# Making the rounded part and the remainder of an activation one group later

## The chip, the cores and the metric

The kernel runs on one core of a Trainium2 chip. A core has a matrix engine (TensorE, PE in the rows, its weight loads PEld), a vector engine (VectorE, DVE), a scalar engine (ScalarE, ACT), GpSimd (POOL) and SyncE (SP), which here only starts transfers. Each engine works through its own queue in order and waits there for the others. The metric is the device time of one execution in microseconds, as the median of several runs. The kernel before took 430.98 us (median of 3 runs, 430.86 to 431.17).

## The reference

A recurrent attention (gates, a running matrix state per head, a normalised read-out) is followed by a two-layer network on its output. Only the network's activation is touched by the change.

```python
# attention, per time step t, for 4 batches and 8 heads, 768 steps, head size 40
C = f_stab * C + i_stab * outer(v_t, k_t)          # state 40x40
n = f_stab * n + i_stab * k_t
y_t = sigmoid(o_t) * (C @ q_t) / max(|n . q_t|, 1)
# network on the 3072 rows of 320 features
h = x @ w_in                                       # 320 -> 2048
g = h * (1.0 / (1.0 + np.exp(-h)))
return (g @ w_out).astype(np.float32)              # 2048 -> 320
```

## The kernel before, in words

The attention is cut into 24 units (12 chunks of 64 time steps, two pairs of batches). Three units make one step of the network, so there are 8 steps, called step 0 to step 7 here as `j` in the code. A step has 384 rows and goes over the 2048 hidden features in 16 groups of 128 (`fc`). While step j of the network runs, the three units of step j+1 are computed in between: `PLACES` says behind which groups their matrix work, the "block", stands (groups 2, 7 and 12 in step 1, groups 0, 4 and 8 in later ones). Step 7 has no units left to compute beside it.

Precision is kept by splitting a value in two parts that TensorE reads at full rate: a rounded part ("hi", type fp32r) and the remainder ("lo"). From step 1 on both layers use three products of such parts. For one group of step j:

- `mm1` (L849): 8 matmuls into `ph`, one of two PSUM buffers.
- `act`: ScalarE makes `th = tanh(ph/2)` (L856), VectorE makes `th = (th + 1) * ph` (L871), ScalarE rounds it to `gh` (L876), VectorE makes the remainder `gl = th - gh` (L880). `th` has two buffers, `gh` and `gl` three each.
- `mm2` (L901): for each of three row tiles three matmuls, gh with hi weights, gh with lo weights, gl with hi weights. It runs two groups behind (`LAG = 2`): the queue of TensorE is mm1(fc), the block if there is one, mm2(fc-2), mm1(fc+1), mm2(fc-1) and so on.

In step 1 `act` also carries pieces of the splitting of the weights (`splits`, L316 to L328): a rounding on ScalarE and a subtraction on VectorE (L318 for w_out, 640 columns, L327 for w_in, 512 columns), up to two in a group. Where a group has a block, a marker on ScalarE stands behind the tanh, for which the second half of the block's L637 matmuls waits, and VectorE has the weighting and the norm (`close`, L576, L655 to L660) ahead of the remainder. Two and three groups behind a block stand, on VectorE, the additions to the state (L757), on ScalarE the gate (L522) and the exponential `lq` (L529), and on GpSimd the multiplication `qt` (L533) that waits for `lq`; later the split of the transposed rows (`xh` on ScalarE L805, `xl` on VectorE L806).

The order on every engine is the order in which the code is written; the scheduler is set to manual for all of them. In step 7 the last group's mm2 order is written out at the end of the program: the three last groups, 13, 14 and 15, one row tile at a time, in the order (13,0) (14,0) (13,1) (14,1) (13,2) (15,0) (15,1) (14,2) (15,2). The rows of a tile are halved and stored right behind it (L919, L921, L926).

Of the kernel before, what the change touches and what calls it, by code (L numbers as in the profile page):

```python
# [8 lines left out]
F32 = mybir.dt.float32  # L9
# [5 lines left out]
ALU = mybir.AluOpType  # L15
# [10 lines left out]
NFC = DFF // 128  # L26
# [3 lines left out]
NSTEP = NU // UPS  # L30
# [13 lines left out]
def mlstm_mlp_kernel(  # L44
# [12 lines left out]
    nc = tc.nc  # L57
# [23 lines left out]
    for k in range(2):  # L81
        m = mask[k * L : (k + 1) * L]
        nc.gpsimd.affine_select(
            out=m, in_=m, compare_op=ALU.is_ge, fill=NEG, base=0,
# [79 lines left out]
    def gates(lo, hi):  # L164

        init = NEG if lo == 0 else m_t[:, lo - 1 : lo]
        nc.vector.tensor_tensor_scan(
            m_t[:, lo:hi], f_t[:, lo:hi], i_t[:, lo:hi], init, op0=ALU.add, op1=ALU.max
        )
        yield  # L170
        l1 = max(lo, 1)
        tt = nc.vector.tensor_tensor
        tt(out=f_t[:, l1:hi], in0=f_t[:, l1:hi], in1=m_t[:, l1 - 1 : hi - 1], op=ALU.add)
        yield
        tt(out=f_t[:, l1:hi], in0=f_t[:, l1:hi], in1=m_t[:, l1:hi], op=ALU.subtract)
        nc.vector.tensor_scalar(f_t[:, l1:hi], f_t[:, l1:hi], -120.0, None, op0=ALU.max)
        if lo == 0:
            nc.vector.memset(f_t[:, 0:1], 0.0)
        yield
        nc.vector.tensor_tensor_scan(  # L180
            LF[:, lo:hi], pat[:, lo:hi], f_t[:, lo:hi], 0.0, op0=ALU.mult, op1=ALU.add
        )
        yield
        tt(out=i_t[:, lo:hi], in0=i_t[:, lo:hi], in1=m_t[:, lo:hi], op=ALU.subtract)
        tt(out=i_t[:, lo:hi], in0=i_t[:, lo:hi], in1=LF[:, lo:hi], op=ALU.subtract)
        yield
# [196 lines left out]
    class Unit:  # L383
# [412 lines left out]
        def xput(self, st):  # L796
# [10 lines left out]
                out=lo, in0=px[:, a, :], in1=hi.bitcast(F32), op=ALU.subtract  # L807
            )

    class Step:  # L810


# [40 lines left out]
        def act(self, fc, splits=(), first=lambda: None, between=lambda: None):  # L853
            j, ph = self.j, self.ph
            th = p2.tile([128, NT], F32, tag="th", name=f"th{j}_{fc}")
            nc.scalar.activation(th, ph, AF.Tanh, scale=0.5)  # L856
            first()
            for x in splits:
                next(x)
            if j == 0:  # L860

                g = p3.tile([128, NT], F32, tag="gh", name=f"g{j}_{fc}")
                nc.vector.scalar_tensor_tensor(
                    out=g, in0=th, scalar=1.0, in1=ph, op0=ALU.add, op1=ALU.mult
                )
                self.g[fc] = (g, None)
                for x in splits:
                    next(x, None)
                between()
                return  # L870
            nc.vector.scalar_tensor_tensor(  # L871
                out=th, in0=th, scalar=1.0, in1=ph, op0=ALU.add, op1=ALU.mult
            )
            gh = p3.tile([128, NT], F32R, tag="gh", name=f"gh{j}_{fc}")
            gl = p3.tile([128, NT], F32R, tag="gl", name=f"gl{j}_{fc}")
            nc.scalar.copy(gh, th)  # L876
            for x in splits:
                next(x, None)
            between()
            nc.vector.tensor_tensor(  # L880
                out=gl, in0=th, in1=gh.bitcast(F32), op=ALU.subtract
            )
            self.g[fc] = (gh, gl)

        def mm2(self, fc, tiles=range(UPS)):
            j = self.j
# [117 lines left out]
    late = [gates(4 * L, 8 * L), gates(8 * L, S)]  # L1004
# [253 lines left out]
```

## Time and profile before

| | us |
|---|---|
| median of the timed runs | 430.98 |
| profiled execution | 431.02 |
| its span, first to last instruction | 429.2 |
| PE busy (5062 matmuls) | 422.4 (98%) |
| PEld busy | 391.7 (91%) |
| DVE busy | 288.5 (67%) |
| ACT busy | 220.6 (51%) |
| POOL busy | 124.8 (29%) |

The shares are means over the whole span. TensorE is busy nearly throughout; the other engines are busier in the first third than later. What counts for a change on the other engines is whether TensorE, which works through its queue without a pause, finds `gh`, `gl` and a free `ph` when it comes to them.

### The profile page before, as it was taken

Reading aid. Unit: us, or ns where it says so; the run is one execution under the profiler, and the core shown is the slowest. Engines: PE = TensorE matmul, PEld = TensorE weight load, DVE = VectorE, ACT = ScalarE, POOL = GpSimd, SP = SyncE. Lnnn points to the kernel's source line nnn. Section 1 sums busy time; section 2 is a strip of 40 time slices with the busy share of each in tenths; the row PEclk is TensorE's granted clock in tenths of the full one; section 3 lists DMA queues with packets and bytes.
Section 4 is the critical chain, followed back from the end, with each engine's and each line's share of the span. In section 5 each row is a group of like instructions: output and inputs, shape, how many; then the busy total and the mean of one; then the engine's idle time right before and its main releaser. Section 6 shows DMA issues by size and latency. Waiting matters only on the chain.

```text
span 429.2 us, 12518 instructions
## 1 busy us (share of the span) xinstructions
PE 422.4 (98%) x5062; PEld 391.7 (91%) x5062; DVE 288.5 (67%) x650; ACT 220.6 (51%) x481; POOL 124.8 (29%) x135
## 2 busy tenths in 40 slices
PE   8999999999999999999999999999999999999995
PEld 4767677899999999999999999999999999999995
DVE  5888799877887677467765677566764756443342
ACT  7684866755755454454454644444454543353331
POOL 5734135234234423043412344034320400000000
PEclk9999999999999999999999999999999999999999
DMA  8999696334551775127660575316750231001001
GB/s 272 387 366 311 177 299 165 117 89 141 159 169 21 196 196 155 31 61 189 174 172 2 123 218 139 118 25 179 209 163 22 54 94 20 18 9 39 2 2 46
DMA packets 62650, 57.17 MB, mean 133 GB/s; under 512 B 31440, under 2 KB 49184, under 8 KB 62592
## 3 DMA queue, kind: packets, MB, share of 16 engines
q1 hardware_dynamic: 62288, 55.94, 45.7%
q8 instruction: 40, 0.66, 0.7%
q10 hardware_dynamic: 208, 0.26, 0.2%
q0 software_dynamic: 96, 0.16, 0.1%
q14 instruction: 18, 0.15, 0.1%
HBM read 48.99 MB, written 7.36 MB: 131 GB/s over the span
## 4 chain that ended last, share of the span: by engine, by line
PE 80%; issue 17%; DVE 1%; ACT 1%; POOL 0%; POOLq 0%; ACTq 0%; DVEq 0%
PE ph L849 35%; PE pout L901 33%; PE p L549 3%; PE p L637 2%; PE p L620 2%; PE dummy L999 1%; PE pu_u L705 1%; PE pu_h L705 1%; DVE D L576 0%; PE e L396 0%; PE px L794 0%; PE pu L717 0%; PE po L604 0%; PE p L794 0%; POOL qt L533 0%
## 5 line engine op out<-in xcount | busy, mean ns | idle before, releaser
L856 ACT ACTIVATE th<-ph 128x384 f32<-128x384 f32 x128 | 62.4, 488 | 106.7 <-PE ph L849 106.2
L849 PE MATMUL ph<-xh,wh 128*128 128x384 f32 x336 | 113.8, 339 | 0.0
L849 PE MATMUL ph<-xl,wh 128*128 128x384 f32 x336 | 113.6, 338 | 0.0
L901 PE MATMUL pout<-woh,gh 128*128 128x320 f32 x336 | 105.5, 314 | 0.0
L901 PE MATMUL pout<-woh,gl 128*128 128x320 f32 x336 | 103.9, 309 | 0.0
L901 PE MATMUL pout<-wol,gh 128*128 128x320 f32 x336 | 103.3, 307 | 0.0
L876 ACT CAST gh<-th 128x384 fp32r<-128x384 f32 x112 | 57.5, 513 | 81.3 <-DVE th L871 69.9
L880 DVE TENSOR_TENSOR gl<-th,gh 128x384 fp32r<-128x384 f32 x112 | 64.6, 577 | 47.5 <-ACT gh L876 47.5
L871 DVE SCALAR_TENSOR_TENSOR th<-th,ph 128x384 f32<-128x384 f32 x112 | 61.4, 548 | 51.1 <-ACT th L856 50.6
L849 PE MATMUL ph<-xh,wl 128*128 128x384 f32 x224 | 75.9, 339 | 0.0
L747 POOL TENSOR_TENSOR Cm<-Cm,lq 40x328 f32<-40x328 f32 x40 | 30.6, 764 | 114.6 <-PE p L637 111.8
L901 PEld LDWEIGHTS pout<-woh,gh 128*128 128x128 f32 x336 | 63.0, 188 | 0.9
L849 PEld LDWEIGHTS ph<-xh,wh 128*128 128x128 f32 x336 | 63.1, 188 | 0.2
L849 PEld LDWEIGHTS ph<-xl,wh 128*128 128x128 f32 x336 | 63.0, 188 | 0.2
L901 PEld LDWEIGHTS pout<-woh,gl 128*128 128x128 f32 x336 | 63.0, 188 | 0.1
L901 PEld LDWEIGHTS pout<-wol,gh 128*128 128x128 f32 x336 | 63.1, 188 | 0.0
L533 POOL TENSOR_TENSOR qt<-qk,lq 104x512 f32<-104x512 f32 x22 | 29.7, 1348 | 99.4 <-ACT lq L529 89.3
L849 PEld LDWEIGHTS ph<-xh,wl 128*128 128x128 f32 x224 | 42.1, 188 | 0.0
L901 PE MATMUL pout<-wo,g 128*128 128x320 f32 x96 | 28.7, 435 | 0.0
L516 POOL TENSOR_TENSOR D<-D,am 128x512 f32<-128x512 f32 x20 | 26.1, 1303 | 4.0 <-DMA D<-LFd 2.5
L508 POOL TENSOR_TENSOR am<-mask,aT 128x512 f32<-128x512 f32 x20 | 24.1, 1205 | 6.6 <-DVE aT L207 5.1
L576 DVE TENSOR_TENSOR D<-p,D 128x512 f32<-128x512 f32 x24 | 16.5, 689 | 13.7 <-PE p L637 12.3
(136 smaller groups left out, 524.4 us busy)
## 6 DMA issues: line engine op xcount, KB each, us to landing
qk<-in_qk_dram SPq DMA_DIRECT2D x24, 512.0 KB, 5.1
ko<-in_ko_dram SPq DMA_DIRECT2D x24, 320.0 KB, 5.3
wro<-in_w_out_dram SPq DMA_DIRECT2D x8, 640.0 KB, 7.3
D<-LFd SPq DMA_DIRECT2D x40, 128.0 KB, 3.1
lq<-LFd SPq DMA_DIRECT2D x40, 128.0 KB, 4.9
wri<-in_w_in_dram SPq DMA_DIRECT2D x8, 512.0 KB, 6.0
vb<-in_vp_dram SPq DMA_DIRECT2D x48, 82.0 KB, 5.1
out_dram<-ob SPq DMA_DIRECT2D x45, 80.0 KB, 2.1
```

What stands on the lines that cost most here:

```text
L508: nc.gpsimd.tensor_tensor(out=self.am, in0=mask.unsqueeze(1).broadcast_to([128, H, L]), in1=aT[:, self.c, self.p, :].unsqueeze(2).broadcas ...
L516: nc.gpsimd.tensor_tensor(out=self.Dm, in0=self.Dm, in1=self.am, op=ALU.add)
L533: nc.gpsimd.tensor_tensor(out=self.qt, in0=self.q[:KS], in1=self.lq[:KS], op=ALU.mult)
L549: nc.tensor.matmul(self.ps[d * L : (d + 1) * L, a * 4 + j, :], self.k[r, d * 4 + j, :], self.q[r, d * 4 + j, :], start=True, stop=True,)
L576: nc.vector.tensor_tensor(out=self.Dm, in0=self.ps, in1=self.Dm, op=ALU.mult)
L747: nc.gpsimd.tensor_tensor(out=v, in0=v, in1=self.lq[r, :, L - 1].unsqueeze(2).broadcast_to([D, H, D1]), op=ALU.mult,)
L849: nc.tensor.matmul(ph, w, x, start=(i == 0), stop=(i == len(ops) - 1))
L856: nc.scalar.activation(th, ph, AF.Tanh, scale=0.5)
L871: nc.vector.scalar_tensor_tensor(out=th, in0=th, scalar=1.0, in1=ph, op0=ALU.add, op1=ALU.mult)
L876: nc.scalar.copy(gh, th)
L880: nc.vector.tensor_tensor(out=gl, in0=th, in1=gh.bitcast(F32), op=ALU.subtract)
L901: nc.tensor.matmul(self.po[t], g[:, ts], w, start=(fc == 0 and i == 0), stop=(last and i == len(ops) - 1),)
```

## The change

For every group of steps 1 to 7 the instructions that make `gh` and `gl` are no longer issued behind the group's own tanh and activation, but behind those of the next group. A list `behind` holds the one group that waits. The pieces of the weight splitting and the block's `close` stay in the group in which they were, between the two. The last group of the program has no next one: there both pairs are made in a row, group 14's and then group 15's. TensorE's queue and the number of instructions stay as they are.

```diff
--- before.py
+++ after.py
@@ -807,6 +807,8 @@
                 out=lo, in0=px[:, a, :], in1=hi.bitcast(F32), op=ALU.subtract
             )
 
+    behind = []
+
     class Step:
 
 
@@ -871,16 +873,26 @@
             nc.vector.scalar_tensor_tensor(
                 out=th, in0=th, scalar=1.0, in1=ph, op0=ALU.add, op1=ALU.mult
             )
+            self.late(splits, between)
             gh = p3.tile([128, NT], F32R, tag="gh", name=f"gh{j}_{fc}")
             gl = p3.tile([128, NT], F32R, tag="gl", name=f"gl{j}_{fc}")
-            nc.scalar.copy(gh, th)
+            self.g[fc] = (gh, gl)
+            behind[:] = [(th, gh, gl)]
+            if j == NSTEP - 1 and fc == NFC - 1:
+                self.late()
+
+        def late(self, splits=(), between=lambda: None):
+            waiting = behind.pop() if behind else None
+            if waiting:
+                th, gh, gl = waiting
+                nc.scalar.copy(gh, th)
             for x in splits:
                 next(x, None)
             between()
-            nc.vector.tensor_tensor(
-                out=gl, in0=th, in1=gh.bitcast(F32), op=ALU.subtract
-            )
-            self.g[fc] = (gh, gl)
+            if waiting:
+                nc.vector.tensor_tensor(
+                    out=gl, in0=th, in1=gh.bitcast(F32), op=ALU.subtract
+                )
 
         def mm2(self, fc, tiles=range(UPS)):
             j = self.j
```

On VectorE in step 1, around group 9, the kernel before has these instructions (`gl_8` is the remainder of group 8, `th_9` the activation of group 9, `wl` a piece of the weight splitting, `Cm` the state, `xl` the split of transposed rows):

```order
L880 TENSOR_TENSOR gl_8_1723<-th_8_1717,gh_8_1722 128x384
L757 TENSOR_TENSOR Cm_139<-Cm_139,pu_u 40x164
L757 TENSOR_TENSOR Cm_139<-Cm_139,pk_1683 40x164
L757 TENSOR_TENSOR Cm_139<-Cm_139,pu_u 40x164
L757 TENSOR_TENSOR Cm_139<-Cm_139,pk_1683 40x164
L806 TENSOR_TENSOR xl_1496<-px_1530,xh_1495 128x3x128
L871 SCALAR_TENSOR_TENSOR th_9_1765<-th_9_1765,ph_9_1756 128x384
L327 TENSOR_TENSOR wl_1767<-wi_1014,wh 128x512
L880 TENSOR_TENSOR gl_9_1771<-th_9_1765,gh_9_1770 128x384
```

The changed kernel has there, with line numbers shifted by the added lines:

```order
L893 TENSOR_TENSOR gl_7_1680<-th_7_1601,gh_7_1679 128x384
L757 TENSOR_TENSOR Cm_139<-Cm_139,pu_u 40x164
L757 TENSOR_TENSOR Cm_139<-Cm_139,pk_1681 40x164
L757 TENSOR_TENSOR Cm_139<-Cm_139,pu_u 40x164
L757 TENSOR_TENSOR Cm_139<-Cm_139,pk_1681 40x164
L806 TENSOR_TENSOR xl_1494<-px_1528,xh_1493 128x3x128
L873 SCALAR_TENSOR_TENSOR th_9_1763<-th_9_1763,ph_9_1754 128x384
L327 TENSOR_TENSOR wl_1765<-wi_1014,wh 128x512
L893 TENSOR_TENSOR gl_8_1724<-th_8_1715,gh_8_1723 128x384
```

The remainder of group 8 has moved past the state's four additions, the split `xl`, the activation of group 9 and a piece of the weight splitting; where it stood is now the remainder of group 7.

At the end of the program ScalarE has this queue in the kernel before (`ob` is an output tile):

```order
L856 ACTIVATE th_14_6192<-ph_14_6183 128x384
L876 CAST gh_14_6195<-th_14_6192 128x384
L856 ACTIVATE th_15_6217<-ph_15_6208 128x384
L876 CAST gh_15_6220<-th_15_6217 128x384
L921 ACTIVATE ob_6242<-pout_0_5896 128x320
```

and this one in the changed kernel:

```order
L858 ACTIVATE th_14_6190<-ph_14_6181 128x384
L888 CAST gh_13_6170<-th_13_6165 128x384
L858 ACTIVATE th_15_6215<-ph_15_6206 128x384
L888 CAST gh_14_6195<-th_14_6190 128x384
L888 CAST gh_15_6220<-th_15_6215 128x384
L933 ACTIVATE ob_6242<-pout_0_5894 128x320
```

The rounding of group 14 now stands behind the tanh of group 15. VectorE's last instructions are in the changed kernel:

```order
L873 SCALAR_TENSOR_TENSOR th_14_6190<-th_14_6190,ph_14_6181 128x384
L893 TENSOR_TENSOR gl_13_6171<-th_13_6165,gh_13_6170 128x384
L873 SCALAR_TENSOR_TENSOR th_15_6215<-th_15_6215,ph_15_6206 128x384
L893 TENSOR_TENSOR gl_14_6196<-th_14_6190,gh_14_6195 128x384
L893 TENSOR_TENSOR gl_15_6221<-th_15_6215,gh_15_6220 128x384
```

Here too group 14's remainder comes behind the activation of group 15; before, it stood ahead of it.

## Rows read from the trace of the kernel before

**Rows 1.** Waits of TensorE over the span: engine, line, releaser: total, times, longest
```profile
PE dummy L999 <- POOL ident masks.py:199: 1.4, 1, 1.4
...
```
**Rows 2.** Timeline, step 7: group 1's tanh and activation, group 0's first remainder matmul
```profile
382.62 0.49 ACT L856 ACTIVATE th<-ph 128x384 f32<-128x384 f32 x1 [1.10 <-PE ph L849]
...
383.15 0.56 DVE L871 SCALAR_TENSOR_TENSOR th<-th,ph 128x384 f32<-128x384 f32 x1 [1.03 <-ACT th L856]
...
385.38 0.31 PE L901 MATMUL pout<-woh,gl 128*128 128x320 f32 x1
```
**Rows 3.** Timeline, step 1, group 9 on ACT, DVE, POOL; group 8's mm2
```profile
109.74 0.49 ACT L856 ACTIVATE th<-ph 128x384 f32<-128x384 f32 x1 [0.54 <-PE ph L849]
110.12 0.61 ACT L325 CAST wh<-wi 128x512 fp32r<-128x512 f32 x1
111.78 0.51 ACT L876 CAST gh<-th 128x384 fp32r<-128x384 f32 x1 [1.04 <-DVE th L871]
...
112.57 0.62 ACT L529 ACTIVATE lq<-lq 104x512 f32<-104x512 f32 x1
...
111.19 0.55 DVE L871 SCALAR_TENSOR_TENSOR th<-th,ph 128x384 f32<-128x384 f32 x1
111.66 0.69 DVE L327 TENSOR_TENSOR wl<-wi,wh 128x512 fp32r<-128x512 f32 x1
112.32 0.56 DVE L880 TENSOR_TENSOR gl<-th,gh 128x384 fp32r<-128x384 f32 x1
...
113.26 1.30 POOL L533 TENSOR_TENSOR qt<-qk,lq 104x512 f32<-104x512 f32 x1 [4.92 <-ACT lq L529]
...
112.49 0.31 PE L901 MATMUL pout<-woh,gl 128*128 128x320 f32 x1
```
**Rows 4.** Timeline, step 1, group 14 on DVE; group 13's mm2
```profile
127.70 0.82 DVE L318 TENSOR_TENSOR wol<-wo,woh 128x640 fp32r<-128x640 f32 x1
128.43 0.55 DVE L880 TENSOR_TENSOR gl<-th,gh 128x384 fp32r<-128x384 f32 x1
...
128.53 0.31 PE L901 MATMUL pout<-woh,gl 128*128 128x320 f32 x1
```
**Rows 5.** Timeline, the end: group 15 on ACT and DVE, PE's last matmuls
```profile
420.80 0.49 ACT L856 ACTIVATE th<-ph 128x384 f32<-128x384 f32 x1 [1.10 <-PE ph L849]
421.91 0.51 ACT L876 CAST gh<-th 128x384 fp32r<-128x384 f32 x1 [0.62 <-DVE th L871]
...
421.32 0.56 DVE L871 SCALAR_TENSOR_TENSOR th<-th,ph 128x384 f32<-128x384 f32 x1 [1.04 <-ACT th L856]
422.45 0.56 DVE L880 TENSOR_TENSOR gl<-th,gh 128x384 fp32r<-128x384 f32 x1 [0.58 <-ACT gh L876]
...
420.97 0.31 PE L901 MATMUL pout<-woh,gh 128*128 128x320 f32 x1
...
422.73 0.31 PE L901 MATMUL pout<-woh,gh 128*128 128x320 f32 x1
...
423.32 0.31 PE L901 MATMUL pout<-woh,gh 128*128 128x320 f32 x1
```
**Rows 6.** Timeline, steps 0 and 3: DVE beside POOL's multiplication qt
```profile
76.74 2.17 POOL L533 TENSOR_TENSOR qt<-qk,lq 104x512 f32<-104x512 f32 x1 [4.71 <-ACT lq L529]
...
76.99 0.66 DVE L327 TENSOR_TENSOR wl<-wi,wh 128x512 fp32r<-128x512 f32 x1
...
204.36 1.30 POOL L533 TENSOR_TENSOR qt<-qk,lq 104x512 f32<-104x512 f32 x1 [4.22 <-ACT lq L529]
...
204.72 1.36 DVE L806 TENSOR_TENSOR xl<-px,xh 128x384 fp32r<-128x384 f32 x1 [0.74 <-ACT xh L805]
```
**Rows 7.** Timeline, step 3, the block of group 8: tanh and the two L637 halves
```profile
207.53 0.47 ACT L856 ACTIVATE th<-ph 128x384 f32<-128x384 f32 x1
...
207.79 0.42 PE L637 MATMUL p<-Cm,qt 40*64 40x41 f32 x16
...
208.35 0.44 PE L637 MATMUL p<-Cm,qt 40*64 40x41 f32 x16
```

## Prediction

> **What bounds the kernel now.** I read the waits of TensorE first, then the timelines of the steady last step, of step 1 and of the end. The view of waits should tell you whether anything is to be won: its longest entry for TensorE is 1.4 us, at the very start of the program [rows 1], and no entry names `gh`, `gl` or `ph`. TensorE works from its first matmul to its last without waiting for the activation. So freeing ScalarE and VectorE from waits for each other can win nothing by itself, and what remains to be asked is whether TensorE, under the new order, comes to a part of the activation before it is made.
>
> That is a question of distance. mm2(fc) stands behind mm1(fc+2). Before, gh(fc) and gl(fc) are made right behind mm1(fc), so two groups of TensorE's work cover them. Afterwards they come behind the tanh and the activation of group fc+1, with one group as cover. The steps of the change then differ only in how much else stands in that one group.
>
> **The change part by part.** Nothing is added or removed but order: the same roundings and remainders, with the same durations. ScalarE's rounding loses its wait for VectorE, since the activation it reads is a group old; VectorE's remainder loses its wait for the rounding for the same reason. Neither is on TensorE's path, so I carry both at nothing. The buffers: tanh(fc+2) needs the `th` that gl(fc) reads, which it gets as soon as mm2(fc) gets gl(fc) itself; it is not a second term.
>
> *Steady groups.* In step 7 the tanh of group 1 starts at 382.62 and its activation at 383.15 [rows 2]. The next VectorE instruction, now gl(0), can start about 0.47 behind the start of an activation (111.19 to 111.66 in [rows 3]) and takes 0.56: it ends at 384.18. TensorE wants it at 385.38 [rows 2], or a weight load earlier. That leaves about 1 us, and gh(0), done behind the tanh at 383.5, has more. The 13 groups of step 7 whose mm2 stands in the loop cost nothing, nor do the like ones of steps 2 to 6, where I read group by group that the remainder still comes in time; behind the `xl` of those steps, the closest place, ScalarE now runs the gate and `lq` about half a microsecond sooner, which brings the next activation forward.
>
> *What a late part costs.* The end of the program shows one small wait already: gl(15) ends at 422.45 + 0.56 = 423.01, and the matmul behind the one that waits for it starts at 423.32, that is 0.31 after the end [rows 5]. The unhindered pitch is (422.73 - 420.97)/12 = 0.147 us per matmul [rows 5], so that matmul would have stood at 422.73 + 4 x 0.147 - in other words, the wait before is 423.32 - (422.73 + 0.44) = 0.15 us. I use the same rule for new waits: next matmul = end of the part + 0.31.
>
> *Step 1, group 8.* VectorE is full here: state additions, `xl`, the activation of group 9 and a piece of the weight splitting run back to back, and gl(8) now stands at the end of that row, where gl(9) was: 112.32, ending at 112.88 [rows 3]. TensorE wants it at 112.49 [rows 3], the matmul behind at 112.64. It gets there at 112.88 + 0.31 = 113.19: 0.55 us lost. As VectorE has work without a gap up to there, the freed waits do not bring it forward (0.06 at most, the start of the piece at 111.66 plus some 0.6).
>
> *Step 1, group 13.* The same picture behind the next block: gl(13) takes the place of gl(14), 128.43 to 128.98, behind the piece that starts at 127.70 [rows 4]. TensorE wants it at 128.53, the matmul behind at 128.68, and comes to that at 129.29: 0.61 us. Other groups of step 1 have the same row of work with more time around it; some are on time only by tenths, and I carry them at nothing.
>
> *The end.* The tail of TensorE begins with the three matmuls of (13,0), then (14,0) at 420.97 [rows 5]. Before, group 14 was long done by then. Now gh(14) stands behind the tanh of group 15: that starts at 420.80, the next ScalarE instruction can follow 0.38 later (109.74 to 110.12 in [rows 3]), at 421.18, and with 0.51 ends at 421.69. TensorE, 0.31 behind that, starts the second matmul of (14,0) at 422.00 in place of 421.12: 0.88 lost. The third one needs gl(14), which VectorE makes behind the activation of group 15: start 421.32 + 0.47 = 421.79, end 422.35, next matmul at 422.66 in place of 420.97 + 0.44 = 421.41. So the tail is 1.25 us late from there on. gh(15) and gl(15) end as before, at 422.42 and 423.01; TensorE now comes to them at 422.66 + 9 x 0.147 = 423.98, so the old wait of 0.15 goes. Net: 1.25 - 0.15 = 1.10 us. Everything behind it (halving, stores) hangs on TensorE's last matmuls and moves along. A bound from below: none of it can be hidden, as TensorE has only these 27 matmuls left.
>
> *The sum.* 0.55 + 0.61 + 1.10 = 2.26 us. Against the profiled execution's 431.02 us that gives 433.3 us; it stands 0.04 above the median of the timed runs, so I predict 433.2 us. What TensorE loses anywhere is lost for good, since it has no waits into which a delay could vanish.
>
> *The port of VectorE and GpSimd.* One cost is open in step 1. The `xl` of step 3 starts 0.36 after GpSimd's `qt` and takes 1.36 us in place of some 0.56, ending 0.42 after `qt` ends at 205.66 [rows 6]: a VectorE instruction with two inputs in SBUF is held up by it. In step 1 `qt` moves too: it follows `lq`, which follows the rounding, and the rounding no longer waits for the activation. gh(8) can start at about 110.12 + 0.52 = 110.64; before, `lq` came 0.79 behind the rounding's start and `qt` 0.69 behind that [rows 3], so `qt` starts at about 112.12 in place of 113.26, and gl(8) follows at 112.32, 0.20 later. In step 0 a piece of the weight splitting that started 0.25 after `qt` took its plain 0.66, and `qt` took 2.17 instead of 1.30 [rows 6]. 0.20 is nearer to 0.25 than to 0.36, so I take gl(8) as not held up. If it is, it ends at 112.12 + 1.30 + 0.42 = 113.84 in place of 112.88: 0.96 us more, and as much again behind group 13, which has the same instructions.
>
> The Trainium skill, page "SBUF — State Buffer", section "Who interferes with whom", says that a VectorE instruction with two SBUF inputs and a GpSimd instruction that reads SBUF share a port pair as an exclusive lock: whichever issues first has it for its whole instruction and the other fully blocks. The `xl` row agrees with that; the row of step 0, where the later one by its recorded start ran unhindered, does not if recorded starts are taken as issue order. By that rule `qt`, started first, would hold gl(8), and the sum would be 3.2 us for one place and 4.2 us for both.
>
> **The rivals.**
>
> *GpSimd gets the port first.* In one or both of the places of step 1 the remainder is held up by `qt`: 431.0 + 2.26 + 0.96 = 434.2 us, or 435.2 us with both. For it speaks the `xl` row and that my start of `qt` has an uncertainty of a tenth; against it the row of step 0 and that the piece ahead of gl(8) still runs when `qt` arrives.
>
> *Only the end costs.* VectorE reaches gl(8) and gl(13) early enough, say because the subtraction ahead of them has its input sooner, and only the 1.10 us of the tail remain: 432.1 us. Against it: VectorE's row there has no gap in [rows 3] that could close.
>
> *Not slower: a hidden wait in the blocks goes.* The second L637 half of a block waits for a marker on ScalarE behind the tanh. In step 3, group 8, the tanh runs from 207.53 to 208.00, late because ScalarE had waited for VectorE; the first half of L637 ends at 208.21, the second starts at 208.35 [rows 7]. With ScalarE freed, the tanh comes about 0.5 us sooner; if that were TensorE's wait, the four such blocks of steps 2 to 5 would win up to 2.0 us, and the time would be 431.0 + 2.26 - 2.0 = 431.3 us, not slower by what can be told. It decides only where the tanh ends after the first half, 208.21; it ends 0.21 before that, so I give it little.
>
> **How the numbers follow.** Forecast as worked out: 0.60, with its own range 432.7 to 433.6. Port lost in one or both places: 0.20. Only the end: 0.12. Not slower, by the blocks or in a way I do not see: 0.08. The range 432.0 to 434.5 takes in the forecast, the tail-only case and the port in one place, and leaves out the port in both and the last rival. A measurement of this kernel can tell about 0.2%, 0.86 us, from no change: slower means over 431.8 us. That holds for the first three cases, less a little for the tail-only case, which lies only 0.3 us above it: slower 0.89, same 0.08, faster 0.03.
>
> **What would show it.** The waits of TensorE should list `gh` and `gl` as releasers, about 2 us in total in a handful of places: two in step 1, at the first mm2 matmuls of groups 8 and 13, and two at the end, for gh(14) and gl(14), of 0.8 and 0.4 us. In steps 2 to 7 the pitch of the groups should be that of before. ScalarE's wait ahead of the rounding and VectorE's ahead of the remainder should be gone. If `qt` takes over 2 us or the remainder over 1 us in step 1, the port decided. I am wrong if TensorE's tail shows no wait for group 14, if waits of TensorE for `gl` turn up in steps 2 to 6, or if the step 1 pitches stay as they were.

## The result and the profile after

The changed kernel takes 435.89 us (median of 6 runs, 434.61 to 437.29); the kernel before takes 431.4 us (median of 6 runs, 430.86 to 432.8, three of them those given above). The ratio is 1.0091 with a 95% interval of 1.0063 to 1.0119: slower, as forecast, but by about twice the forecast loss and outside the stated range of 432.0 to 434.5. A ratio is estimated from the single runs, so it is not exactly the quotient of the two medians; two executions far slower than the rest, one of 833.57 us in the experiments and one of 437.11 us of the kernel before, are left out of the ratios. The profiled execution takes 435.94 us with a span of 434.2 us.

The view of TensorE's waits, whose only large entry before was the one at the start [rows 1], now reads (total, times, longest):

```profile
PE pout L913 <- DVE gl L893: 2.8, 2, 1.4
PE dummy L1011 <- POOL ident masks.py:199: 1.4, 1, 1.4
PE pout L913 <- ACT gh L888: 0.5, 1, 0.5
PE p L637 <- POOL qt L533: 0.5, 1, 0.5
```

Two waits for a remainder and one for a rounded part: the places are those of the prediction, step 1 twice and the end, but the two remainders cost far more than half a microsecond each. The last line, `qt`, lies ahead of step 1, where the change moves nothing.

What the change was meant to free is freed. The rounding and the remainder have these rows in the kernel before and in the changed one (busy time, mean ns of one, then the idle time of the engine just before them and what ended it; above the dots before, below them after):

```profile
L876 ACT CAST gh<-th 128x384 fp32r<-128x384 f32 x112 | 57.5, 513 | 81.3 <-DVE th L871 69.9
L880 DVE TENSOR_TENSOR gl<-th,gh 128x384 fp32r<-128x384 f32 x112 | 64.6, 577 | 47.5 <-ACT gh L876 47.5
...
L888 ACT CAST gh<-th 128x384 fp32r<-128x384 f32 x112 | 56.8, 507 | 15.6 <-PE p L637 15.4
L893 DVE TENSOR_TENSOR gl<-th,gh 128x384 fp32r<-128x384 f32 x112 | 66.8, 596 | 0.1
```

ScalarE waited 69.9 us in all for the activation and VectorE 47.5 us for the rounded part; both waits are gone but for 0.2 us, and the program is longer all the same.

The timeline of step 1, group 9 (start, length, engine, line), answers to [rows 3]:

```profile
111.98 0.56 DVE L873 SCALAR_TENSOR_TENSOR th<-th,ph 128x384 f32<-128x384 f32 x1
112.45 0.69 DVE L327 TENSOR_TENSOR wl<-wi,wh 128x512 fp32r<-128x512 f32 x1
113.05 1.66 DVE L893 TENSOR_TENSOR gl<-th,gh 128x384 fp32r<-128x384 f32 x1
...
112.85 1.45 POOL L533 TENSOR_TENSOR qt<-qk,lq 104x512 f32<-104x512 f32 x1 [3.71 <-ACT lq L529]
...
113.14 0.30 PE L913 MATMUL pout<-wol,gh 128*128 128x320 f32 x1
114.76 0.41 PE L913 MATMUL pout<-woh,gl 128*128 128x320 f32 x1 [1.32 <-DVE gl L893]
115.01 0.31 PE L913 MATMUL pout<-woh,gh 128*128 128x320 f32 x1
```

VectorE's row stands where it was foreseen. But the remainder of group 8 takes 1.66 us in place of 0.56: `qt` on GpSimd starts 0.20 ahead of it and the remainder ends 0.41 after `qt` ends at 114.30. In group 14, which answers to [rows 4], the same happens:

```profile
130.04 0.82 DVE L318 TENSOR_TENSOR wol<-wo,woh 128x640 fp32r<-128x640 f32 x1
130.77 1.66 DVE L893 TENSOR_TENSOR gl<-th,gh 128x384 fp32r<-128x384 f32 x1
...
130.55 1.47 POOL L533 TENSOR_TENSOR qt<-qk,lq 104x512 f32<-104x512 f32 x1 [4.16 <-ACT lq L529]
...
132.49 0.41 PE L913 MATMUL pout<-woh,gl 128*128 128x320 f32 x1 [1.45 <-DVE gl L893]
132.74 0.31 PE L913 MATMUL pout<-woh,gh 128*128 128x320 f32 x1
```

The end answers to [rows 5]:

```profile
424.67 0.49 ACT L858 ACTIVATE th<-ph 128x384 f32<-128x384 f32 x1 [1.84 <-PE ph L851]
425.06 0.50 ACT L888 CAST gh<-th 128x384 fp32r<-128x384 f32 x1
425.79 0.51 ACT L888 CAST gh<-th 128x384 fp32r<-128x384 f32 x1 [0.22 <-DVE th L873]
...
425.20 0.56 DVE L873 SCALAR_TENSOR_TENSOR th<-th,ph 128x384 f32<-128x384 f32 x1 [1.70 <-ACT th L858]
425.67 1.22 DVE L893 TENSOR_TENSOR gl<-th,gh 128x384 fp32r<-128x384 f32 x2
...
425.62 0.42 PE L913 MATMUL pout<-woh,gh 128*128 128x320 f32 x1 [0.55 <-ACT gh L888]
425.87 0.31 PE L913 MATMUL pout<-wol,gh 128*128 128x320 f32 x1
426.27 0.42 PE L913 MATMUL pout<-woh,gl 128*128 128x320 f32 x1
426.53 0.31 PE L913 MATMUL pout<-woh,gh 128*128 128x320 f32 x1
```

gh(14) comes behind the tanh of group 15 and TensorE waits, then waits again shortly for gl(14). The steady stretch answers to [rows 2]: the remainder now follows the activation directly, and TensorE wants it 1.3 us after its end.

```profile
387.02 0.55 DVE L873 SCALAR_TENSOR_TENSOR th<-th,ph 128x384 f32<-128x384 f32 x1 [1.71 <-ACT th L858]
387.49 0.55 DVE L893 TENSOR_TENSOR gl<-th,gh 128x384 fp32r<-128x384 f32 x1
...
389.31 0.31 PE L913 MATMUL pout<-woh,gl 128*128 128x320 f32 x1
```

A table of where TensorE falls behind can be made from the starts of its matmuls: each is compared with the same matmul of the kernel before, and the differences are taken from one mark to the next. The marks are the first mm1 matmul of step 1 (78.61 before, 79.42 after; nothing that the change moves is executed before it), the first and the last mm2 matmul of group 8 and of group 13 of step 1, the first matmul of the last mm1, and TensorE's last matmul. All in us; the rows below the first belong to the experiments.

| kernel | ahead of step 1 | group 8 | group 13 | all between, to the last mm1 | the end | sum |
|---|---|---|---|---|---|---|
| changed | 0.81 | 1.59 | 1.72 | -0.18 | 1.02 | 4.96 |
| step 1 at once | -0.04 | 0.00 | 0.00 | -0.12 | 1.04 | 0.88 |
| group 14 of step 7 at once | 3.11 | 1.59 | 1.72 | -0.14 | -0.06 | 6.22 |
| both at once | 0.93 | 0.00 | 0.00 | 0.08 | -0.05 | 0.96 |
| remainder ahead of the piece | 1.72 | 0.18 | 0.19 | -0.16 | 1.04 | 2.97 |
| the same, and group 14 at once | 0.80 | 0.17 | 0.19 | -0.06 | -0.06 | 1.04 |
| no qt in the two units | 0.88 | 0.49 | 0.68 | 0.16 | 1.04 | 3.25 |
| qt later | 1.00 | 0.49 | 0.62 | 0.03 | 1.04 | 3.18 |
| remainder first, qt sooner | 0.30 | 1.09 | 1.17 | -0.02 | 1.04 | 3.58 |

The first column differs from execution to execution, by up to 3 us, in a stretch whose instructions no kernel of this list changes; the profiled execution of before lies low in it. It is not a cost of the change: the kernel with both places at once has 0.93 us there and takes the time of the kernel before (below). The change's own loss in its profiled execution is 1.59 + 1.72 - 0.18 + 1.02 = 4.15 us, 0.96% of 431.02 us, in line with the ratio of the timed runs.

### The profile page after: what moved, and what is told of

Read it like the earlier page. It is cut to its first block, busy times and chain, and to the rows that moved or that the text cites. A ratio compares the mean times of both kernels' runs of the same rounds, so it can differ in the third digit from the quotient of the medians.

```text
span 434.2 us, 12495 instructions
## 1 busy us (share of the span) xinstructions
PE 423.0 (97%) x5062; PEld 391.5 (90%) x5062; DVE 283.6 (65%) x650; ACT 212.4 (49%) x481; POOL 125.0 (29%) x135
## 4 chain that ended last, share of the span: by engine, by line
PE 69%; issue 17%; DMA 4%; DVE 4%; ACT 3%; SPq 1%; POOL 1%; POOLq 0%; ACTq 0%; DVEq 0%
PE ph L851 31%; PE pout L913 29%; PE p L549 3%; PE p L637 2%; PE p L620 2%; DMA qk<-in_qk_dram 2%; DMA wro<-in_w_out_dram 1%; DMA ko<-in_ko_dram 1%; PE pu_u L705 1%; DVE gl L893 1%; POOL qt L533 1%; PE pu_h L705 0%; DVE wi L282 0%; DVE wol L318 0%; DVE wo L282 0%
## 5 line engine op out<-in xcount | busy, mean ns | idle before, releaser
L893 DVE TENSOR_TENSOR gl<-th,gh 128x384 fp32r<-128x384 f32 x112 | 66.8, 596 | 0.1
```

Of the source, the lines that this page charges most:

```text
L893: nc.vector.tensor_tensor(out=gl, in0=th, in1=gh.bitcast(F32), op=ALU.subtract)
```

## The experiments

Theory A at this point: the loss sits in three places, and in the two of step 1 most of it is the hold-up by `qt`. All ratios are to the kernel before, run on the same chip, with 95% intervals. Some of these overlap with that of the changed kernel (1.0063 to 1.0119), among them those of "group 14 of step 7 at once", "no qt" and "qt later". What such an edit gives back is read from the traces, by the table above. From TensorE's last matmul to the end of the span it is 4.69 to 4.74 us in every trace, so nothing that TensorE loses is made up for behind that matmul.

**Step 1 at once.**

```diff
-            self.late(splits, between)
+            if j > 1:
+                self.late(splits, between)
             gh = p3.tile(...)
...
             behind[:] = [(th, gh, gl)]
+            if j == 1:
+                self.late(splits, between)
```

> Step 1 makes its rounded parts and remainders at once again, as before; steps 2 to 7 make them a group later. Theory A (the loss sits in three places: groups 8 and 13 of step 1 and the end): in the trace both waits of step 1 are gone, 1.6 and 1.7 us, the wait at the end stays, and from step 1 on TensorE lies about 3.3 us earlier than in the changed kernel; about 432.6 us against 435.9. Theory B (the later order costs something in every step): less than half of that comes back, 434.3 us or more, and the pitch of groups in steps 2 to 6 is longer than in the kernel before.

Measured: 432.55 us against 431.88, ratio 1.0023 (1.0007 to 1.0039). Both waits of step 1 are gone, and the end keeps its 1.04 us, which is 0.24%:

```profile
PE dummy L1014 <- POOL ident masks.py:199: 1.4, 1, 1.4
...
PE pout L916 <- ACT gh L891: 0.5, 1, 0.5
```

Theory A holds; steps 2 to 7 cost nothing (-0.12 in the table), so theory B falls.

**Group 14 of step 7 at once.**

```diff
-            if j == NSTEP - 1 and fc == NFC - 1:
+            if j == NSTEP - 1 and fc >= NFC - 2:
                 self.late()
```

> Only group 14 of step 7 is made at once, so the end of the program has only group 15 left to make. Theory A: TensorE's waits for gh and gl of group 14 go, the small old one for group 15 comes back, 1.0 us less than the changed kernel, 434.9 us; the waits of 1.6 and 1.7 us in step 1 stay. Theory B (the end is hidden by the output transfers): no change, 435.9 us.

Measured: 434.27 us against 431.88, ratio 1.0059 (1.0037 to 1.0081). What the table leaves, 1.59 + 1.72 - 0.14 - 0.06 = 3.11 us or 0.72%, lies within the interval. The end's loss is gone (-0.06), the two waits of step 1 stay:

```profile
PE pout L913 <- DVE gl L893: 2.8, 2, 1.5
...
```

So the end is not hidden by the output transfers: theory A holds, and what TensorE waits there is paid in full. The timed runs show it where step 1 is at once too: 1.0023 with the end's wait (above), 0.9994 without it (next).

**Both at once.** The two edits above together.

> Step 1 and group 14 of step 7 at once, everything between a group later. Theory A: no wait of TensorE for gh or gl beyond the old small one; the time of the kernel before within 0.2%, with no gain, since TensorE had no wait to lose. Theory B (the later order costs in every step): slower than before by 0.5 us or more. Theory C (the freed ScalarE and VectorE win something on TensorE): faster than before by 0.3 us or more.

Measured: 431.55 us, ratio 0.9994 (0.9977 to 1.0010), and no wait for `gh` or `gl` among TensorE's waits. No change: the later order in steps 2 to 7 neither costs nor wins anything, though ScalarE and VectorE wait less for each other there. The interval alone would not exclude the 0.3 us of theory C; the trace does, with 0.08 in the stretch between and -0.05 at the end.

The trace also answers the question of a hidden wait in the blocks. In step 3, group 8, this kernel has:

```profile
208.02 0.49 ACT L858 ACTIVATE th<-ph 128x384 f32<-128x384 f32 x1 [1.31 <-PE ph L851]
...
208.87 0.42 PE L637 MATMUL p<-Cm,qt 40*64 40x41 f32 x16
...
209.42 0.44 PE L637 MATMUL p<-Cm,qt 40*64 40x41 f32 x16
```

The tanh ends 0.36 ahead of the first half of the matmuls, where before it ended 0.21 behind their start [rows 7], and yet the second half follows the first by 0.55 us, against 0.56 before. The tanh was not what that half waited for.

**No qt in units 8 and 9.** Leaves out the multiplication of q by the decay in these two units.

```diff
+            if self.n in (8, 9):
+                nc.scalar.copy(self.qt, self.q[:KS])
+                return
             nc.gpsimd.tensor_tensor(out=self.qt, in0=self.q[:KS], in1=self.lq[:KS], op=ALU.mult)
```

> The changed kernel, but the qt of units 8 and 9 (the two multiplications on GpSimd that overlap the late remainders of step 1) is a plain copy of q by ScalarE: the multiplication with the decay is left out for these two units. Theory A (port): gl(8) and gl(13) take 0.56 instead of 1.66 us, and TensorE's waits shrink to the sizes that VectorE's row alone explains, 0.55 and 0.61 us: 2.0 to 2.1 us less than the changed kernel, about 433.9 us. Theory B (VectorE's full row alone makes the remainders late): no change, 435.9 us.

Measured: 434.05 us against 431.2, ratio 1.0068 (1.0044 to 1.0091). The timeline of group 9:

```profile
113.13 0.55 DVE L896 TENSOR_TENSOR gl<-th,gh 128x384 fp32r<-128x384 f32 x1
...
113.74 0.41 PE L916 MATMUL pout<-woh,gl 128*128 128x320 f32 x1 [0.22 <-DVE gl L896]
```

With GpSimd silent there, the remainder takes 0.55 us, and the losses are 0.49 and 0.68 us, against 0.55 and 0.61 in the prediction. The rest of the 1.59 and 1.72, namely 1.10 and 1.04 us, is `qt`: theory A.

**qt later.** All work stays and some is added.

```diff
             if self.c > 0:
+                if self.n in (8, 9):
+                    for _ in range(3):
+                        nc.scalar.copy(identb, ident)
                 self.look()
                 self.near()
```

> The changed kernel with all its work, but ScalarE makes three short copies (0.2 to 0.3 us each) ahead of the exponential that qt of units 8 and 9 waits for, so qt starts about 0.6 us later, behind the start of the late remainder. Theory A (the port goes to the one that asks first): the remainder takes 0.56 us, qt waits for it, 2.0 us less than the changed kernel, about 433.9 us, although work was added. Theory B (qt and the remainder share the port, whoever comes first): the remainder stays at 1 us or more and less than half of it comes back.

Measured: 433.64 us against 431.2, ratio 1.0058 (1.0039 to 1.0077):

```profile
113.26 0.55 DVE L896 TENSOR_TENSOR gl<-th,gh 128x384 fp32r<-128x384 f32 x1
...
113.90 1.31 POOL L533 TENSOR_TENSOR qt<-qk,lq 104x512 f32<-104x512 f32 x1 [4.56 <-ACT lq L529]
...
113.86 0.41 PE L916 MATMUL pout<-woh,gl 128*128 128x320 f32 x1 [0.23 <-DVE gl L896]
```

Three copies on ScalarE that rewrite a tile with what it holds, 0.95 us in all, give back 1.10 us in each of the two places, as much as leaving `qt` out. Here `qt` starts only after the remainder has ended, so the run shows that the meeting is what costs, and not which of the two goes first when they meet; that is for the next runs.

**Remainder ahead of the piece.** In a group that has both pieces and a block, the remainder also moves ahead of the block's `close`.

```diff
-            for x in splits:
-                next(x, None)
-            between()
+            if not splits:
+                between()
             if waiting:
                 nc.vector.tensor_tensor(
                     out=gl, in0=th, in1=gh.bitcast(F32), op=ALU.subtract
                 )
+            for x in splits:
+                next(x, None)
+            if splits:
+                between()
```

> All later as in the changed kernel, but where a group carries pieces of the weight splitting, the remainder of the group before stands ahead of the pieces' subtraction on VectorE, not behind it. Theory A (the remainder is late because of the piece, and because GpSimd's qt gets the port behind the piece): gl(8) starts about 0.6 us sooner, ahead of qt, and takes 0.56 instead of 1.66; both waits in step 1 are gone, the one at the end stays, about 3.3 us less than the changed kernel, 432.6 us. Theory B (qt holds the remainder wherever it stands): the remainder still takes over 1 us and 1 us at most comes back.

Measured: 432.51 us against 431.88, ratio 1.0019 (1.0004 to 1.0033):

```profile
113.67 0.55 DVE L892 TENSOR_TENSOR gl<-th,gh 128x384 fp32r<-128x384 f32 x1
114.14 1.80 DVE L327 TENSOR_TENSOR wl<-wi,wh 128x512 fp32r<-128x512 f32 x1
...
113.76 1.62 POOL L533 TENSOR_TENSOR qt<-qk,lq 104x512 f32<-104x512 f32 x1 [3.71 <-DVE th L873]
...
114.06 0.30 PE L916 MATMUL pout<-wol,gh 128*128 128x320 f32 x1
114.27 0.41 PE L916 MATMUL pout<-woh,gl 128*128 128x320 f32 x1
114.53 0.31 PE L916 MATMUL pout<-woh,gh 128*128 128x320 f32 x1
```

The remainder starts 0.09 ahead of `qt` and runs unhindered, as theory A has it, while the piece behind it now takes 1.80 us, which no one waits for. The losses shrink to 0.18 and 0.19 us. They are not gone, although that had been expected: even unhindered the remainder ends a little late (114.22 + 0.31 = 114.53).

**The same, and group 14 at once.**

> Remainder ahead of the weight pieces, and group 14 of step 7 at once. Theory A: every loss is gone and nothing is won: the time of the kernel before within 0.2%, as in the kernel with step 1 and group 14 at once. Theory C (freeing ScalarE and VectorE wins something on TensorE): 0.3 us or more faster than before.

Measured: 432.70 us against 431.2, ratio 1.0026 (1.0011 to 1.0041). The table explains 0.17 + 0.19 us of it, 0.08%; the interval begins at 0.11%. What the rest is stays open; the trace of this kernel has no further wait behind the start of step 1. Nor does the microsecond that group 14 gives back in this trace (-0.06 at the end against 1.04) show in the timed runs, which are no faster than the 1.0019 of the kernel without that edit, run on another chip. Neither the changed order nor any mix of it beat the kernel before.

**Remainder first, qt sooner.** On top of the kernel with the remainder ahead of the piece:

```diff
         def misc(self):
+            if self.n in (8, 9):
+                self.look()
+                self.near()
+                self.gate()
+                return
             self.gate()
```

> The kernel with the remainder ahead of the weight piece, and in units 8 and 9 the exponential and qt stand ahead of the gate, so qt starts about 0.37 us sooner: some 0.2 to 0.3 us ahead of the remainder by the recorded starts, while the instruction ahead of the remainder on VectorE (the activation, one input in PSUM) leaves the port free. Theory D (what held the remainder in the changed kernel was the line: the piece ahead of it had the port, qt came to wait for it and was next): with no one on the port, a remainder recorded 0.2 us behind qt still gets it first, as the piece of step 0 did at 0.25; gl(13) takes 0.56 us, at 0.3 it is on the edge for gl(8). Theory E (the one whose recorded start is first has the port): both remainders take over 1 us, and TensorE waits 1 us more in each place, about 434.3 us against 432.5 without the exchange.

Measured: 435.07 us against 431.45, ratio 1.0073 (1.0051 to 1.0095). The two remainders and their `qt`:

```profile
112.25 1.47 DVE L897 TENSOR_TENSOR gl<-th,gh 128x384 fp32r<-128x384 f32 x1
...
111.99 1.31 POOL L533 TENSOR_TENSOR qt<-qk,lq 104x512 f32<-104x512 f32 x1 [3.35 <-ACT lq L529]
...
129.38 1.57 DVE L897 TENSOR_TENSOR gl<-th,gh 128x384 fp32r<-128x384 f32 x1
...
129.22 1.31 POOL L533 TENSOR_TENSOR qt<-qk,lq 104x512 f32<-104x512 f32 x1 [3.80 <-ACT lq L529]
```

`qt` starts 0.26 and 0.16 ahead, with VectorE's instruction before the remainder reading one input from PSUM, and both remainders are held until `qt` is done; the loss rises from 0.18 and 0.19 to 1.09 and 1.17 us. Theory D, on which I had put the hold-up down to the piece that had the port, falls. Theory E fits all the remainders: the one recorded first goes first, and 0.16 is enough. The two do not share here: `qt` keeps its plain 1.31 us, and the remainder ends 0.42 us behind it. One row of step 0 does not fit theory E either; the next section comes to it.

## Why the prediction was wrong

The sign, the three places and the mechanism of the sum were right: TensorE had no wait to lose, one group of cover suffices in steps 2 to 7 up to the end, and what arrives late is lost in full. What failed is a term that the prediction saw and carried at nothing. Term by term:

- *The end*, 1.10 us forecast: 1.02 measured, 1.08 to 1.10 removed by making group 14 at once. (The "4 x 0.147" in the working is a slip; three matmuls, 0.44, lie between the two starts, and the 0.15 us of the old wait is worked out with that.)
- *Group 8 and group 13 by VectorE's row alone*, 0.55 and 0.61: 0.49 and 0.68, 0.49 and 0.62 in the two runs in which `qt` is out of the way. The rule "end of the part + 0.31" held in each of them, as in the changed kernel: 114.71 + 0.31 = 115.02, and the row says 115.01.
- *Everything else*, nothing: -0.18 us in all.
- *The port of VectorE and GpSimd*, carried at nothing: 1.10 and 1.04 us. This is the step that failed. The place and the start of `qt` had been worked out rightly (0.20 ahead of the remainder), and the price nearly so (0.96 us each, where `qt` itself then took 1.45 and 1.47 us in place of 1.30). The sign that the prediction named for it, a remainder of over 1 us in step 1, is there. What was wrong was the sentence "0.20 is nearer to 0.25 than to 0.36, so I take gl(8) as not held up". It set one row of step 0 against the `xl` row of step 3 and read a threshold of distance into the two. There is none in that range: remainders 0.26, 0.22, 0.20 and 0.16 behind `qt` were held, and one 0.09 ahead of it was not. The trace of before also had more rows on the one side than the prediction weighed: in steps 2 to 6 nine `xl`, all 0.35 to 0.36 behind a `qt`, took 1.36 to 1.37 us, and in step 1 two pieces 0.94 and 0.95 behind one took 0.92 and 1.03 in place of 0.69 and 0.82.

With both hold-ups the prediction had 435.2 us, to which it gave a part of 0.20. In the trace the change's own loss is 4.15 us, where that rival has 4.18; the profiled execution lies 0.7 above 435.2, which is the 0.81 us ahead of step 1. By the rule of the Trainium skill, page "SBUF — State Buffer", section "Who interferes with whom", the one that issues first has the shared port pair and the other fully blocks; the remainder behind `qt` (1.66 us) and the piece behind it in the other order (1.80 us) agree with it, as far as recorded starts tell the order of issue. In this case the rule was the better guide than the single row of step 0.

That single row is not explained. It is there in the changed kernel too, in step 0:

```profile
77.57 2.14 POOL L533 TENSOR_TENSOR qt<-qk,lq 104x512 f32<-104x512 f32 x1 [4.73 <-ACT lq L529]
...
77.79 0.66 DVE L327 TENSOR_TENSOR wl<-wi,wh 128x512 fp32r<-128x512 f32 x1
```

The piece starts 0.22 behind `qt`, runs its plain 0.66 us, and `qt` takes 2.14. It is so in all ten traces: the piece starts 0.15 to 0.25 behind `qt` and takes 0.66 us, and `qt` takes 2.06 to 2.18. The remainders that were held lie at 0.16 to 0.26, and in "remainder first, qt sooner" the VectorE instruction ahead of them is of the same kind as in step 0, an activation with one input in PSUM. So neither the distance nor the instruction ahead nor the order of recorded starts explains it; what is different in step 0 stays open.

The rival of a hidden wait in the blocks is wrong: in the kernel with both places at once the tanh comes sooner, the matmuls behind it do not, and nothing was won. That only the end costs was wrong as well.

## What to carry to other kernels

When an engine's queue is reordered, look not only at when the moved instruction is done, but at which instructions of other engines move with it: here the freed ScalarE brought GpSimd's multiplication forward by over a microsecond (1.20 us in group 9, measured against TensorE's matmuls), straight in front of the one VectorE instruction that had become urgent. Where the rows show two engines that hold each other up for a whole instruction, carry the meeting in the sum, at the price of the one that comes second, and don't set it to nothing on one exception. And where the bounding engine has no waits, making its inputs later can win nothing and may cost: first at the last items of the program, which have the least work ahead of them to hide behind.

## What the runs showed of the hardware that I had not expected

Added work can take time off: three copies on ScalarE, 0.95 us together, took 2.2 us off the changed kernel's two places (1.10 in each), only by starting `qt` later. The trace shows it; the timed ratios, 1.0058 and 1.0091, have intervals that overlap.

The distance at which the hold-up can decide is small: 0.16 us between recorded starts cost a 0.56 us instruction another 1.0 us. And its size can be worked out beforehand. A held VectorE instruction ends, counted from the end of `qt`, its own length less 0.14 us later: 0.41 for the remainders and `xl` (plain 0.55), 0.55 for the piece of 512 columns (0.69), 0.68 for that of 640 (0.82). The last two are from "remainder ahead of the piece". So next to nothing of it is done while `qt` runs.
